# Conversions further behind their loads, and the first gated weights loaded in part, in a fused attention, expert and gated-MLP kernel

## The chip, the cores and the metric

The kernel runs on one core of a Trainium2 chip. The metric is the device time of one execution in microseconds, the median of several runs. Engines are named as in the profile: PE is TensorE (matmuls), PEld its weight loads, DVE VectorE, ACT ScalarE, POOL GpSimd (`G` in the code), SP SyncE, whose queue issues nearly all DMAs. Every engine works through its own queue in program order.

## What is computed

```python
state = f[:, :, t, :, None] * state + np.einsum('bhd,bhe->bhde', k[:, :, t], v[:, :, t])   # f = sigmoid(f_logit), 768 steps
y[:, :, t] = np.einsum('bhd,bhde->bhe', q[:, :, t], state)                                 # 4 batches, 8 heads of 48
...
x = attn_out.transpose(0, 2, 1, 3).reshape(B * S, H * D)            # 3072 tokens of 384
expert_idx = np.argmax(logits, axis=1)                              # 8 experts, cosine logits / tau
gate_w = probs[np.arange(N), expert_idx]
out[mask] = gate_w[mask, None] * (np.maximum(x[mask] @ w1[e], 0.0) @ w2[e])   # 384 -> 1024 -> 384
...
return ((x @ w_a) * (x @ w_b) @ w_out).astype(np.float32)           # 384 -> 1536 -> 384
```

All of it is in fp32. The inputs of the last step arrive as 64-bit floats.

## The kernel before

A product in fp32 is made of three matmuls: each operand is split into a high part (a rounded copy, on ACT) and a low part (the difference, on POOL or DVE), and the products high x high, low x high and high x low are added in PSUM. There are three stages. Attention and routing take the first 145 us or so; the tokens are scattered to slots in order of their expert.

**The expert loop** (L1367 on) runs `s` from 0 to 63: 8 experts of 8 steps (`FJ`). A step makes a block of hidden units (`h_part(s)`: 9 matmuls on lines 1212 to 1214, then `hh` on ACT and `hl` on DVE), adds the block of two steps before to the output (`y_part(s - 2)`: 9 matmuls, L1255) and, three times per expert, transposes tokens of the next one (`x_turn`, L1202; the two parts of `a` on ACT L1205 and DVE L1206). After an expert's last block its output is copied from PSUM to `yT` (DVE L1271, ACT L1273); the next expert's first output matmul into the same PSUM bank waits for that. `w_more(s)` loads the experts' weights into `raw` (L878) and splits them (L886 to L895).

Beside this, `prep_run(s)` (L1096) prepares the gated MLP's weights a little at a time: first what `defer` has put down for this step, then `loads()`, then the two streams `combines()` and `conv()`, as far as a budget of microseconds goes.
- `conv()` turns 18 pieces of 768 KB from 64 to 32 bits: three of `w_out`, six of `w_a`, six of `w_b`, three of `w_out`. A piece takes ACT L948 and DVE L950, L951 (into `ct`), L954 and a last operation (L957 or L987). `loads()` loads a piece into a free part of `big` and notes the step from which it may be converted. Converted `w_out` is split (ACT L963, POOL L964) and stored to `wost` (L969).
- `combine(0)` and `combine(1)` make 15 combined blocks each of `w_a` and `w_b` (sums on DVE L999; a scheme that needs 23 and not 27 block products), split them (ACT L1032, POOL L1035) and store them to `wst` in DRAM (L1055).

**The visits** (L1528 on): `P = at // 8` runs over the units of the gated MLP, 8 per tile of 512 tokens. A unit reads two chunks of `wst` (1024 and 896 KB, `w_chunk`, L1075), which go through a ring of three buffers `WR`; the ring lies in the two weight tiles of the last experts' ring that the last expert's pieces use first. A visit is 6 matmuls (L1456; `c2` has 3) and one or two additions of PSUM into `big` (DVE L1466, L1469, L1472, or ACT). Half of the visits of a unit fall into the next P (`late` in `SLOTS`), so P0 reads only nine of the fifteen rows: 0, 1 and 4 to 7 of chunk 0, and 2 to 4 of chunk 1. From P3 on the matmuls with `w_out` (L1485, L1487, L1489) run between the visits; their left operand is the product a * b (DVE L1433, split by ACT L1437 and POOL L1438). `x_prep` makes the 15 sums of x for a tile of tokens (L1347, split on L1355 and L1360): the first tile's within the last steps of the expert loop, on DVE, the others in the visits, on POOL. The gates (L1288 to L1311: a power on POOL, then short DVE operations) need the logits, which one DMA of 40-byte rows brings (L1542). The last two `y_part` run at visits 0 and 1. Every third visit calls `prep_run(64 + at // 3)`.

## Time and profile before

| what | value |
|---|---|
| median of 3 runs | 818.62 us (815.15 to 819.36) |
| the profiled execution | 818.64 us |
| its span, first to last instruction | 816.6 us |
| mean granted clock of TensorE | 0.984 of 2.4 GHz |
| busy: PE, PEld | 772.1 us (95%), 742.9 us |
| busy: DVE, ACT, POOL | 596.9 (73%), 420.5 (52%), 412.4 us (51%) |
| DMA | 226.8 MB, 278 GB/s over the span |

The span is one execution by the profiler; the time is that of the same execution and about 2 us longer. A timeline row gives the start, the length (of a group that runs together) and, in brackets, how long the engine was idle before it and what ended that. For SP the length of a group holds the waits between its issues. A stretch's `PEclk` is the mean granted clock: 1.00 is 2.4 GHz, 0.50 is 1.2 GHz.

### The profile page before, as it was taken

How to read it: one execution, taken by the hardware profiler on the slowest of the kernel's cores; microseconds unless marked ns; L12 is line 12 of the kernel's file. 1: busy time of each engine (PE TensorE's matmuls, PEld its weight loads, DVE VectorE, ACT ScalarE, POOL GpSimd, SP SyncE). 2: the span in 40 equal slices, each digit the busy share in tenths (PEclk: the TensorE clock that was granted, in tenths of full speed). 3: DMA queues.
4: the chain of work that ended last, by engine and by line, in shares of the span. 5: the costliest groups of instructions: out<-in, count | busy, mean ns of one | idle time of the engine just before them, and what ended most of it. 6: DMA issues, size and time to landing. Idle time of an engine off the chain costs nothing.

```text
span 816.6 us, 16783 instructions
## 1 busy us (share of the span) xinstructions
PE 772.1 (95%) x6354; PEld 742.9 (91%) x6354; DVE 596.9 (73%) x1007; ACT 420.5 (52%) x889; POOL 412.4 (51%) x392
## 2 busy tenths in 40 slices
PE   7899989789999999997899999999999999999995
PEld 5899988779989999996789999999999999999994
DVE  7999995689878957784798657866756765686552
ACT  5899973555657656643344344443434433444331
POOL 6667763353578746960455253436316535333313
PEclk9999999889999999998999999999999999999999
DMA  7989742988489987967998899789888888988982
GB/s 276 334 286 338 247 155 92 290 262 272 164 239 293 304 265 199 270 192 221 345 379 299 318 324 329 277 322 334 292 303 328 309 293 318 335 293 295 334 316 67
DMA packets 83087, 226.82 MB, mean 278 GB/s; under 512 B 10649, under 2 KB 42247, under 8 KB 76727
## 3 DMA queue, kind: packets, MB, share of 16 engines
q1 hardware_dynamic: 79639, 216.10, 78.3%
q0 software_dynamic: 3072, 9.56, 3.0%
q8 instruction: 52, 0.85, 0.4%
q14 instruction: 36, 0.29, 0.1%
q10 hardware_dynamic: 288, 0.02, 0.0%
HBM read 192.95 MB, written 32.70 MB: 276 GB/s over the span
## 4 chain that ended last, share of the span: by engine, by line
PE 61%; DVE 20%; DMA 9%; issue 5%; POOL 2%; ACT 2%; SPq 0%; DVEq 0%; POOLq 0%; ACTq 0%
PE pv L1456 20%; PE po L1255 8%; PE pw L1456 5%; PE pq L1489 5%; PE pq L1487 5%; PE pq L1485 5%; DMA raw<-moe_w 4%; DMA w<-wst 2%; PE ph L1212 2%; DVE Rt L241 2%; PE ph L1214 2%; PE ph L1213 2%; DVE big L1472 2%; DVE big L1433 2%; DVE a L1355 2%
## 5 line engine op out<-in xcount | busy, mean ns | idle before, releaser
L1438 POOL TENSOR_TENSOR w<-big,w 128x512 fp32r<-128x512 f32 x72 | 94.2, 1321 | 176.6 <-ACT w L1437 172.3
L1456 PE MATMUL pv<-w,w 128*128 128x256 f32 x912 | 136.6, 285 | 12.4 <-DMA w<-wst 6.9
L1472 DVE TENSOR_TENSOR big<-big,pv 128x512 f32<-128x512 f32 x144 | 98.3, 683 | 60.9 <-PE pv L1456 60.8
L1456 PEld LDWEIGHTS pv<-w,w 128*128 128x128 f32 x912 | 127.1, 190 | 17.0 <-DVE big L1466 5.2
L1456 PE MATMUL pv<-a,w 128*128 128x256 f32 x816 | 122.1, 283 | 0.2
L1456 PEld LDWEIGHTS pv<-a,w 128*128 128x128 f32 x816 | 115.0, 189 | 1.8 <-DVE big L1466 1.0
L895 POOL TENSOR_TENSOR w<-raw,w 128x512 fp32r<-128x512 f32 x48 | 78.4, 1654 | 42.2 <-ACT w L892 41.8
L1489 PE MATMUL pq<-raw,w 128*128 128x384 f32 x288 | 97.1, 337 | 1.6 <-POOL w L1438 1.6
L1485 PE MATMUL pq<-raw,w 128*128 128x384 f32 x288 | 97.2, 337 | 0.0
L1487 PE MATMUL pq<-raw,w 128*128 128x384 f32 x288 | 96.8, 336 | 0.0
L1255 PE MATMUL po<-hh,w 128*128 128x224 f32 (+7 forms) x384 | 84.7, 357 | 5.1 <-DVE yT L1271 4.2
L1466 DVE TENSOR_TENSOR big<-big,pv 128x256 f32<-128x256 f32 x96 | 40.3, 420 | 50.7 <-PE pv L1456 48.9
L1255 PEld LDWEIGHTS po<-hh,w 128*128 128x128 f32 x384 | 69.7, 199 | 7.7 <-DVE yT L1271 4.9
L1433 DVE TENSOR_TENSOR big<-big 128x512 f32<-128x512 f32 x72 | 65.3, 934 | 1.7
L1212 PE MATMUL ph<-a,w 128*128 128x224 f32 (+7 forms) x192 | 66.2, 345 | 0.0
L1214 PE MATMUL ph<-a,w 128*128 128x224 f32 (+7 forms) x192 | 65.9, 343 | 0.0
L1213 PE MATMUL ph<-a,w 128*128 128x224 f32 (+7 forms) x192 | 65.9, 343 | 0.0
L1437 ACT ACTIVATE w<-big 128x512 fp32r<-128x512 f32 x72 | 44.9, 633 | 38.7 <-DVE big L1433 38.7
L1463 ACT ACTIVATE big<-pw 128x256 f32<-128x256 f32 x48 | 18.4, 383 | 78.7 <-PE pw L1456 73.9
L1235 ACT ACTIVATE hh<-ph 128x224 fp32r<-128x224 f32 (+7 forms) x64 | 31.4, 491 | 49.7 <-PE ph L1214 49.4
L1489 PEld LDWEIGHTS pq<-raw,w 128*128 128x128 f32 x288 | 54.2, 188 | 2.2 <-POOL w L1438 2.2
L1485 PEld LDWEIGHTS pq<-raw,w 128*128 128x128 f32 x288 | 54.4, 189 | 0.6 <-ACT w L1437 0.6
(275 smaller groups left out, 1732.2 us busy)
## 6 DMA issues: line engine op xcount, KB each, us to landing
w<-wst SPq DMA_DIRECT2D x49, 1024.0 KB
w<-wst SPq DMA_DIRECT2D x49, 896.0 KB
raw<-wost SPq DMA_DIRECT2D x72, 384.0 KB
raw<-moe_w SPq DMA_DIRECT2D x32, 768.0 KB
qkf<-qkf SPq DMA_DIRECT2D x20, 768.0 KB
wst<-big SPq DMA_DIRECT2D x21, 512.0 KB
vx<-vx SPq DMA_DIRECT2D x24, 192.0 KB
big<-moe_w_out SPq DMA_DIRECT2D x6, 768.0 KB
```

The source lines that it names most:

```text
L895: (G if i < NPOOL else V).tensor_tensor(out=wt[:, 1, f], in0=raw[:, f], in1=wt[:, 0, f].bitcast(F32), op=ALU.subtract)
L1212: T.matmul(out=out, lhsT=wh, rhs=xh, start=first, stop=False)
L1213: T.matmul(out=out, lhsT=wl, rhs=xh, start=False, stop=False)
L1214: T.matmul(out=out, lhsT=wh, rhs=xl, start=False, stop=last)
L1255: T.matmul(out=OS[e][k], lhsT=w[:, j % 4, k * 128:(k + 1) * 128], rhs=x, start=(j == 0 and w is wh and x is hh), stop=(j == FJ - 1 and x i ...
L1433: V.tensor_tensor(out=a, in0=a, in1=b, op=ALU.mult)
L1438: G.tensor_tensor(out=g[:, 1], in0=a, in1=g[:, 0].bitcast(F32), op=ALU.subtract)
L1456: T.matmul(out=out, lhsT=wt, rhs=xt_, start=first and j == 0, stop=j == 2, skip_group_check=True)
L1472: V.tensor_tensor(out=o, in0=o, in1=bank, op=ALU.subtract)
L1485: T.matmul(out=q, lhsT=gh, rhs=wh, start=(f == 0), stop=False)
L1487: T.matmul(out=q, lhsT=gh, rhs=wl, start=False, stop=False)
L1489: T.matmul(out=q, lhsT=gl, rhs=wh, start=False, stop=(f == F2J - 1))
```

## The change

- `loads()`: a piece may be converted 5 steps after its load in the first expert, 3 in the others and 8 (of three visits each) in the visits, in place of 3 everywhere.
- Converted `w_out`: split and store one step later in the loop (2 and 3 steps behind). The last three pieces are split into tiles of the `a` ring that are free by then and not into a part of `big`, and the two pauses of 9 us of budget behind each are gone.
- The last three pieces of `w_out` may be loaded when `combine(1)` comes to its last block (phase 3.5), not when it has ended.
- `combine` ends two steps behind its last block and not three.
- `w_chunk(0)` loads six rows (768 KB, two DMAs) at s = 60, `w_chunk(1)` three rows (384 KB) at s = 62, each ahead of the step's `h_part`; chunk 2 is loaded whole after `combine(1)`, as before. Before, all three were loaded whole at that point.
- `x_prep` makes its sums two ahead of the split in place of one. The first tile's runs two per step from s = 57 and one in each visit, not three per step from s = 58.
- The gate logits are loaded at visit 9, not 2; the gates run on even visits 22 to 40, not 16 to 34.

```diff
-                if not at or (waiting[0] == (2, 1) and phase[0] < 4):
+                if not at or (waiting[0] == (2, 1) and phase[0] < 3.5):
...
-                ready.append((now[0] + 3, i) + waiting.pop(0))
+                ready.append((now[0] + (5 if now[0] < FJ else 3 if now[0] < NE * FJ else 8), i) + waiting.pop(0))
...
-                    to = part[n if n < 3 else 5].bitcast(F32R).rearrange("p (i j d) -> p i j d", i=2, j=2)
+                    to = (part[n].bitcast(F32R) if n < 3 else flat(X[NE - 1][n % 2])).rearrange("p (i j d) -> p i j d", i=2, j=2)
...
-                    defer(1, split)
-                    defer(2, store)
+                    lag = 2 if now[0] < NE * FJ else 1
+                    defer(lag, split)
+                    defer(lag + 1, store)
                     take(i, 2)
-                    if n >= 15:
-                        for _ in range(2):
-                            yield 9.0
...
             for i in range(NR):
+                if (w, i) == (1, NR - 1):
+                    free[5], phase[0] = now[0] + 1, 3.5
...
-            until = now[0] + 3
+            until = now[0] + 2
...
         def w_chunk(h):
-            if h < 2 * (NTT * NU + 1):
+            if h < 2:
+                for lo, hi in ((0, 2), (4, 8)) if h == 0 else ((2, 5),):
+                    SP.dma_start(out=WR[h][:, lo:hi].bitcast(F32), in_=wst[h, :, lo:hi])
+            elif h < 2 * (NTT * NU + 1):
...
-            for h in range(3):
-                w_chunk(h)
+            w_chunk(2)
...
             sums(0)
+            sums(1)
...
-                sums(o + 1)
+                sums(o + 2)
...
         for s in range(NE * FJ):
             e, j = divmod(s, FJ)
+            if s in (NE * FJ - 4, NE * FJ - 2):
+                w_chunk((s + 4 - NE * FJ) // 2)
...
-            if s == IDS + 1:
+            if s == IDS:
                 x_more()
-            if s > IDS:
-                for _ in range(3):
+            if s >= IDS:
+                for _ in range(2):
                     next(x_first, None)
...
+                next(x_first, None)
-            if at == 2:
+            if at == 9:
                 SP.dma_start(out=idf, in_=heads[0:NT].rearrange("(t p) w -> p t w", p=128))
-            if at == 16:
+            if at == 22:
...
-            if at >= 16 and at % 2 == 0 and at <= 34:
+            if at >= 22 and at % 2 == 0 and at <= 40:
```

How this moves instructions shows at three places. (Line numbers of the changed kernel are up to six higher; numbers behind names tell buffers apart.) The first is DVE's queue in the first expert, around the flag `flag_b`; `ct` and `big` are the two halves of a conversion, `a` the transposed tokens, `w` a weight split. Before:

```order
L1236 SCALAR_TENSOR_TENSOR hl<-ph,hh 128x224
L950 TENSOR_SCALAR ct<-ct 128x768
L951 TENSOR_SCALAR ct<-ct 128x768
L1162 TENSOR_REDUCE fl_94<-srt 1x1
L1163 TENSOR_SCALAR fl_94<-fl_94 1x1
L1164 TENSOR_SCALAR fl_94<-pcs 1x1
L1165 TENSOR_REDUCE flag_i<-fl_94 1x1
L1166 CAST flag_b<-flag_i 1x1
L1206 TENSOR_TENSOR a_2541<-pt,a_2540 128x448
L1236 SCALAR_TENSOR_TENSOR hl<-ph,hh 128x224
L954 SCALAR_TENSOR_TENSOR big<-big,ct 128x768
L957 SCALAR_TENSOR_TENSOR big<-big 128x768
```

and now, from `flag_b` on:

```order
L1169 CAST flag_b<-flag_i 1x1
L1209 TENSOR_TENSOR a_2541<-pt,a_2540 128x448
L1239 SCALAR_TENSOR_TENSOR hl<-ph,hh 128x224
L887 TENSOR_TENSOR w_2524<-raw,w_2524 128x512
L1209 TENSOR_TENSOR a_2541<-pt,a_2540 128x448
L1239 SCALAR_TENSOR_TENSOR hl<-ph,hh 128x224
L951 TENSOR_SCALAR ct<-ct 128x768
L952 TENSOR_SCALAR ct<-ct 128x768
L1209 TENSOR_TENSOR a_2541<-pt,a_2540 128x448
L1239 SCALAR_TENSOR_TENSOR hl<-ph,hh 128x224
L955 SCALAR_TENSOR_TENSOR big<-big,ct 128x768
L958 SCALAR_TENSOR_TENSOR big<-big 128x768
```

The first half of the first conversion, which stood ahead of the first `a`, stands behind the second, and its second half behind the third. From the first `a` to the copy of the first output `yT`, 18 rows further on, there are two whole conversions now and there were two and a half.

The second is DVE's queue ahead of the copy of expert 1's output (`yT`, 432 columns). Before, and then now:

```order
L1236 SCALAR_TENSOR_TENSOR hl<-ph,hh 128x416
L999 TENSOR_TENSOR yT_2534<-yT_2534,yT_2532 128x512
L999 TENSOR_TENSOR yT_2533<-yT_2532,yT_2534 128x512
L954 SCALAR_TENSOR_TENSOR big<-big,ct 128x768
L895 TENSOR_TENSOR w_66<-raw,w_66 128x512
L1236 SCALAR_TENSOR_TENSOR hl<-ph,hh 128x416
L1264 TENSOR_LOAD off_i
L1264 ISA x2
L1271 ISA
L1271 COPY yT_2533<-po 128x432
```

```order
L1034 TENSOR_TENSOR big<-yT_2533,big 128x4x128
L895 TENSOR_TENSOR w_66<-raw,w_66 128x512
L1239 SCALAR_TENSOR_TENSOR hl<-ph,hh 128x416
L1267 TENSOR_LOAD off_i
L1267 ISA x2
L1274 ISA
L1274 COPY yT_2533<-po 128x432
L998 TENSOR_TENSOR yT_2534<-yT_2534,yT_2532 128x512
L998 TENSOR_TENSOR yT_2533<-yT_2532,yT_2534 128x512
L955 SCALAR_TENSOR_TENSOR big<-big,ct 128x768
```

The two sums (L999, now L998) stood ahead of the copy and stand behind it.

The third is SP's queue at the end of the expert loop: stores of b's sums to `wst`, loads of chunks (`w_2524<-wst`, elements per partition), of 64-bit pieces (`moe_w_out`), of converted `w_out` (`raw<-wost`) and of the logits (`heads`). Before:

```order
L1055 DMA wst<-big 128x3x256
L1055 DMA wst<-big 128x256
L1055 DMA wst<-big 128x4x256
L1075 DMA w_2524<-wst 128x2048
L1075 DMA w_2524<-wst 128x1792
L1075 DMA w_2524<-wst 128x2048
L1428 DMA raw<-wost 128x768 x2
L1542 DMA yT_2534<-heads 128x24x10
L925 DMA big<-moe_w_out 128x2x768
L1075 DMA w_2524<-wst 128x1792
L1075 DMA w_2524<-wst 128x2048
L1075 DMA w_2524<-wst 128x1792
```

and now:

```order
L1076 DMA w_2524<-wst 128x512
L1076 DMA w_2524<-wst 128x1024
L1054 DMA wst<-big 128x3x256
L1054 DMA wst<-big 128x256
L926 DMA big<-moe_w_out 128x2x768
L1054 DMA wst<-big 128x4x256
L1076 DMA w_2524<-wst 128x768
L1079 DMA w_2524<-wst 128x2048
L926 DMA big<-moe_w_out 128x2x768
L1433 DMA raw<-wost 128x768 x2
L1079 DMA w_2524<-wst 128x1792
L1079 DMA w_2524<-wst 128x2048
```

Three loads in part (512 and 1024, then 768) stand among the stores, two conversion loads stand ahead of chunk 3 (1792), and the logits have gone behind chunk 4 (2048); behind that come two stores to `wost`, a third conversion load and the logits, and only then chunk 5.

## Rows read from the trace of the kernel before

**Rows 1.** The page, busy us, share of the span and instructions of TensorE.

```profile
PE 772.1 (95%) x6354; PEld 742.9 (91%) x6354; DVE 596.9 (73%) x1007; ACT 420.5 (52%) x889; POOL 412.4 (51%) x392
```

**Rows 2.** Busy us by stretch: PE, PEld, DVE, ACT, POOL, granted clock, DMA.

```profile
460.00:800.00 340.00, 339.66 (x2502) 337.03 (x2501) 223.46 (x368) 137.18 (x287) 139.46 (x128) 1.00 0.86 310
```

**Rows 3.** Waits of PE, whole run: us in total, times, longest.

```profile
PE pv L1456 <- DMA w<-wst: 6.9, 2, 4.7
PE pt L1202 <- DVE a L1206: 5.3, 3, 3.7
PE po L1255 <- DVE yT L1271: 4.2, 2, 3.1
```

**Rows 4.** PE's timeline: start, length, line, operation, [idle before <- releaser].

```profile
159.80 1.01 PE L1202 MATMUL pt<-ident,yT 112*128 112x112 f32 x4 [3.66 <-DVE a L1206]
178.89 2.23 PE L1255 MATMUL po<-hh,w 128*128 128x448 f32 x5 [3.14 <-DVE yT L1271]
...
241.59 1.22 PE L1255 MATMUL po<-hh,w 128*128 128x416 f32 x5 [1.06 <-DVE yT L1271]
```

**Rows 5.** DVE's timeline, 156 to 179 us.

```profile
156.31 0.56 DVE L950 TENSOR_SCALAR ct<-ct 128x768 f32<-128x768 f32 x1 [1.59 <-ACT ct L948]
156.91 1.65 DVE L951 TENSOR_SCALAR ct<-ct 128x768 int32<-128x768 int32 x1
...
159.14 0.60 DVE L1206 TENSOR_TENSOR a<-pt,a 128x448 fp32r<-128x448 f32 x1
...
159.97 0.94 DVE L954 SCALAR_TENSOR_TENSOR big<-big,ct 128x768 int32<-128x768 int32 x1
160.94 0.96 DVE L957 SCALAR_TENSOR_TENSOR big<-big 128x768 int32<-128x768 int32 x1
...
178.46 0.38 DVE L1271 COPY yT<-po 128x224 f32<-128x224 f32 x1
```

**Rows 6.** ACT's timeline, the split of the raw piece.

```profile
165.75 0.63 ACT L886 ACTIVATE w<-raw 128x512 fp32r<-128x512 f32 x1 [0.71 <-DMA raw<-moe_w]
```

**Rows 7.** Busy us by stretch, the three at low clock (columns as rows 2).

```profile
158.50:165.30 6.80, 5.50 (x27) 5.50 (x28) 6.24 (x15) 4.23 (x10) 1.86 (x1) 0.51 0.89 196
...
376.90:383.70 6.80, 6.16 (x21) 6.19 (x22) 0.00 (x0) 0.60 (x1) 0.00 (x0) 0.50 0.94 374
394.00:397.40 3.40, 3.40 (x19) 3.40 (x18) 1.41 (x3) 0.38 (x1) 0.00 (x0) 0.51 0.97 405
```

**Rows 8.** PE's timeline, end of the expert loop and first visits.

```profile
367.51 1.31 PE L1255 MATMUL po<-hh,w 128*128 128x384 f32 x6 [0.82 <-ACT hh L1235]
...
377.54 1.62 PE L1456 MATMUL pv<-w,w 128*128 128x256 f32 x6 [4.67 <-DMA w<-wst]
...
393.42 0.59 PE L1456 MATMUL pv<-w,w 128*128 128x256 f32 x3 [2.20 <-DMA w<-wst]
...
403.24 0.98 PE L1456 MATMUL pv<-w,w 128*128 128x256 f32 x6 [1.58 <-DVE big L1466]
...
404.77 0.88 PE L1456 MATMUL pv<-w,w 128*128 128x256 f32 x6
```

**Rows 9.** SP's timeline: issues, their length with the waits among them.

```profile
354.99 14.94 SPq L1055 DMA_DIRECT2D wst<-big  x6
370.02 6.08 SPq L1075 DMA_DIRECT2D w<-wst  x3
...
442.07 4.07 SPq L969 DMA_DIRECT2D wost<-big  x2
```

**Rows 10.** DMA packets, 376 to 382 us.

```profile
DMA packets 410, 2.40 MB, mean 400 GB/s; under 512 B 47, under 2 KB 47, under 8 KB 260
```

**Rows 11.** Busy us, first to sixth P with output matmuls (columns as rows 2).

```profile
404.77:452.57 47.80, 44.67 (x317) 41.95 (x316) 43.77 (x73) 23.08 (x50) 25.91 (x23) 1.00 0.92 340
```

**Rows 12.** DVE's and POOL's timelines, two operations of the gates.

```profile
400.57 1.83 DVE L1291 TENSOR_TENSOR yT<-yT,gm 128x192 f32<-128x192 f32 x1
...
388.75 4.56 POOL L1288 TENSOR_TENSOR gm<-yT,half 128x24 f32<-128x24 f32 x1 [19.22 <-DMA yT<-heads]
```

More of the change, by code (lines that the diff above doesn't have):

```diff
@@ L904, in build @@
         now = [0]
+        flat = lambda t: t.rearrange("p a b -> p (a b)")
         due, tail = [], []
@@ L1316, in build @@
         QS = {}
-        flat = lambda t: t.rearrange("p a b -> p (a b)")
         XS = [flat(wring[2 + i // 6])[:, (i % 6) * 512:(i % 6 + 1) * 512] for i in range(12)]
```

## The prediction

> **What bounds the kernel now.** I read the page first: TensorE is busy 772.1 of 816.6 us [rows 1], so nearly all a change can win lies in the 44 us in which it isn't, and in the stretches where it runs at half clock. The table by stretches shows where that isn't: from 460 us on TensorE is busy 339.66 of 340 us at full clock [rows 2]. Whatever the change does to the work there is worth nothing unless it makes another engine the bound. So I looked at the waits of TensorE over the whole run [rows 3]: the longest single ones are for a chunk of gated weights (4.7), for the transposed tokens `a` (3.7) and for the output copy `yT` (3.1). The timelines put each in its place [rows 4, 8]. Last, the granted clock around them: after the stalls at 156 and 373 us TensorE ran at 1.2 GHz for 6.8 us each, and again for 3.4 us at 394 [rows 7]. A stretch at half clock loses half its length: 3.4, 3.4 and 1.7 us. The profiled execution took 818.64 us, its span 816.6; the median of the three runs is 818.62, so sums against the profiled one need no correction. Anything under 0.5% (4.1 us) can't be told from no change here.
>
> **First conversion two steps later (157 to 179 us).** DVE's in-order queue holds the first conversion's two `ct` operations (0.56 and 1.65 us) ahead of the first `a` copy, and they could only start at 156.31 because their piece had just landed [rows 5]. TensorE waits 3.66 us for that copy [rows 4]. In the new order both stand behind two `a` copies, so this stall goes, and with it the half-clock stretch (3.4). That is 7.1 us at 165 us, but not at the end: the next hard point is the first matmuls of expert 1's output, which wait for the copy of expert 0's `yT` at 178.46 [rows 4, 5]. Between `a` and that copy DVE still does two whole conversions in place of two and a half (0.94 and 0.96 us go, and some waiting on ACT), and one weight split that needs a raw piece which lands at 165.75 [rows 6] whatever DVE does, since its load was issued long before. From 159.14 to 178.84 are 19.7 us; from an `a` copy at about 156.0 (when its transposes are done; ACT's half of the copy stands behind the same conversion now) I take off the 1.9 us and some 1.1 of the waits, but keep 0.5 for the landing: 156.0 + 17.2 + 0.5 = 173.7, TensorE restarts at 174.3 instead of 178.89. TensorE will have come there early and still stalls, for about as long as now, so I count no gain of clock there. **Term: -4.5** (-3 if the split waits longer on the raw piece, -6 if the copy comes as soon as DVE's work allows).
>
> **Expert 1's copy ahead of two sums (241 us).** TensorE's 1.06 us wait for `yT` [rows 4] ends behind two sums of the combination that now stand behind the copy. **Term: -1.1** (0 to -1.1: the same time may come back as a wait for weights).
>
> **End of the expert loop (367 to 405 us).** Now: TensorE finishes its outputs at 372.87 and waits 4.67 us for chunk 0 [rows 8], which SP issued only at 370.02, after the last store of b's sums [rows 9]. From 372.87 to the first visit with output matmuls at 404.77 are 31.9 us. Of these 4.67, 2.20 and 1.58 are the stalls [rows 8], 5.1 half of 6.8 and 3.4 at half clock [rows 7]: 18.35 us are left, the work at full clock. After: chunk 0's six rows go at the sixtieth step of the loop, when SP has the last but one group of b stores out, and chunk 1's three at the sixty-second; 768 KB at the 400 GB/s of [rows 10] is 2 us, so both are there when TensorE comes. That is at 372.05, since the 0.82 us wait at 367.51 [rows 8] (ACT's copy behind x preparation) goes with x prepared two steps instead of three per turn. What is late next is chunk 3. Chunk 2 still has to wait for the last store of b: its issue ended at 369.93, and SP stood with the three chunk loads until 376.10 [rows 9], so about 5.9 us to land. Behind chunk 2 in SP's new order come a 768 KB conversion load, two of 384 KB and chunk 3 with 896 KB: 3.54 MB at 400 GB/s from 375.8 is 384.6. TensorE wants it after its two outputs, P0 and half of P1, about 10 of the 18.35 us: 382. So 2.6 us of wait, and I add 1.4 for chunk 5, which now stands behind a pair of stores, the third conversion load and the gate logits: 372.05 + 18.35 + 4.0 = 394.4 for what is now at 404.77. **Term: -10.4.** Bounds: -14.4 with no new wait, -7 if the waits are twice mine less some overlap, or another half-clock stretch follows.
>
> What a store costs before its bytes can be read has a rival price. The Trainium skill, "DMA: Bandwidth & Descriptors", section on the anatomy of one DMA, fits a DMA (on GpSimd's path) as 2.0 us plus the bytes at 436 GB/s; for the last 512 KB store that estimate is 3.2 us where this trace shows 5.9. By the page chunk 2 would go 2.7 us sooner, chunk 3 would not be late, and the sum would be that of rival 2 below.
>
> **Visits with output matmuls, until DVE is rid of conversions (405 to 453 us).** DVE is busy 43.77 of 47.80 us there, TensorE 44.67 [rows 11]: DVE sets the pace. Two conversions lie in it now, one of them after the change (the second is done ahead): 0.56 twice, 0.94 and 0.96 [rows 5], 3.0 us less (with both `ct` operations at the cheap price; 1.65 is the dear one). Against it the gates, six visits later, bring their dear product of 1.83 us [rows 12] into it, with its short neighbours some 2.2 more. **Term: -0.9** (+3 if the pile of gates and third conversion holds one more visit, -3 if the gates find room).
>
> Moved at no cost: GpSimd's power for the gates (4.56 us, [rows 12]), six or seven visits later, with nobody waiting for it in that stretch; split copies of converted w_out into spare `a` tiles; x sums two ahead. Were their cover gone, that is GpSimd held by the power, they cost up to 4.6 us of late `w` splits, which is in the +3 end above and the slower rival.
>
> **Sum:** 4.5 + 1.1 + 10.4 + 0.9 = 16.9; 818.64 - 16.9 = **801.7**. Its own range, with the ends above partly cancelling, is 797 to 807.
>
> **Rivals.** (1) *DMA takes half of the late gain.* Chunks 3 and 5 come 5.2 us (half of 10.4) later than I said, and expert 1's output restarts at 176.8 and not 174.3, 2.5 more. For it: in 376 to 382 us the DMA engines already move 400 GB/s with no rest [rows 10]. Against it: 0.8 MB of chunks 0 and 1 is no longer loaded at all, and the other 1.1 MB goes two to four steps earlier. 801.7 + 7.7 = 809.4. (2) *Stores land sooner* now that no chunk load shares the queue with the last of them: chunk 3 comes in time and its 2.6 us go, 799.1. For it: what landed in 5.9 us had 1.9 MB of chunk loads on its heels, and now has 0.4. Against it: most of those loads can only have moved once the store was through. (3) *It does not do what it says*: chunk 0's part stands on SP until all stores of b have landed, as it does now, so the 10.4 goes; and expert 1's output waits for the raw piece until 178.9, so the 4.5 goes: 816.6. Against it: the rows it reads were stored by earlier steps. (4) *Slower: SP is held by the stores of converted w_out.* SP issues in order; such a pair held it 4.07 us at 442.07 [rows 9], when GpSimd was late with the split. In the new order pairs stand ahead of chunk 5, chunk 7 and a later one, with GpSimd's 4.56 us power in between. A chunk that is issued 4.07 late needs 2.3 us to load (896 KB at 400 GB/s) with TensorE waiting, and 1.7 of half clock after it: 8.1 us each, 24.2 for three, 825.9. It decides from 7.0 us each on (21 us, up to 822.7). Against it: in the new order the first two splits on GpSimd come right after the last split of the sums, ahead of the power, so only the third can be late.
>
> **How the numbers follow.** Forecast 0.54 (801.7); (1) 0.20 (809.4); (2) 0.10 (799.1); (3) 0.10 (816.6); (4) 0.06 (825.9). Faster by over 0.5% (under 814.5) is the first three: 0.84; the same 0.10; slower 0.06. The range reaches from 796 to 814: it takes in the forecast's own range, (1) and (2) but for their tails, and leaves out (3) and (4) and about 0.04 below.
>
> **What would show it.** Right: the wait of TensorE for `a` at 156 us is under 0.5 us, the one for `yT` stays between 3 and 4.5 us and ends at 173 to 176; the 241 us wait is gone; chunk 0 has landed before TensorE ends the outputs; the first output matmul of the visits starts 15 to 20 us earlier than now in the trace (10.4 + 5.6); waits for `w<-wst` are left, on chunks 3 and 5, 2 to 5 us in all; the distance from 404.77 to 452.57 is 47 us, and from there to the end unchanged. Wrong: the chunk waits add up to over 8 us, or DVE's stretch grows by over 4, or half clock turns up in a new place.

## The result: 0.65% slower

| | before | after |
|---|---|---|
| median of 20 runs each | 818.22 us (814.67 to 819.58) | 823.62 us (817.22 to 827.04) |
| ratio of the runs | | 1.0065, 95% interval 1.0046 to 1.0084 |
| the profiled execution, its span | 818.64, 816.6 us | 824.94, 822.9 us |

The forecast was 801.7 us, the range 796 to 814. The page of the changed kernel, TensorE's busy time and its clock in 40 slices:

```profile
PE 774.3 (94%) x6354; PEld 744.5 (90%) x6354; DVE 602.5 (73%) x1007; ACT 419.9 (51%) x889; POOL 406.5 (49%) x392
...
PEclk9999999989999999999898999999999999999999
```

TensorE's waits over the whole run (us in all, times, longest):

```profile
PE pv L1461 <- DMA w<-wst: 6.1, 1, 6.1
PE pv L1461 <- DVE big L1477: 5.6, 4, 3.3
PE po L1258 <- ACT yT L1276: 5.1, 2, 4.9
PE pv L1461 <- DVE big L1471: 4.7, 4, 2.9
...
PE pt L1205 <- DVE a L1209: 2.1, 1, 2.1
```

Against [rows 3] the waits for `a` have gone from 5.3 to 2.1 us, and two kinds stand at the top that were small: TensorE waits for DVE's additions (L1471, L1477), that is for a free bank. The timeline of TensorE has them, with the wait in brackets:

```profile
174.69 1.82 PE L1258 MATMUL po<-hh,w 128*128 128x448 f32 x3 [4.93 <-ACT yT L1276]
...
281.44 0.56 PE L1205 MATMUL pt<-ident,rows 100*128 100x100 f32 x4 [2.08 <-DVE a L1209]
...
373.93 0.98 PE L1461 MATMUL pv<-w,w 128*128 128x256 f32 x6 [0.82 <-DVE hl L1239]
...
398.69 0.98 PE L1461 MATMUL pv<-w,w 128*128 128x256 f32 x3 [6.10 <-DMA w<-wst]
...
412.14 1.32 PE L1461 MATMUL pv<-w,w 128*128 128x256 f32 x6 [2.91 <-DVE big L1471]
...
434.37 1.01 PE L1461 MATMUL pv<-w,w 128*128 128x256 f32 x3 [3.35 <-DVE big L1477]
```

[Rows 4] answer to the first, [rows 8] to the third and fourth. Behind each of these waits but that of 0.82 at 373.93 the clock falls (busy us by stretch, columns as in rows 2; the granted clock is the third number from the end):

```profile
174.69:181.00 6.31, 6.31 (x17) 5.28 (x18) 6.21 (x7) 2.46 (x5) 4.25 (x3) 0.54 1.02 304
283.00:288.00 5.00, 5.00 (x20) 4.91 (x20) 4.45 (x7) 1.70 (x5) 0.99 (x1) 0.67 0.90 184
398.60:402.10 3.50, 3.42 (x16) 3.45 (x17) 1.72 (x3) 0.63 (x2) 0.00 (x0) 0.50 0.95 299
412.00:416.00 4.00, 3.86 (x17) 3.86 (x18) 2.40 (x6) 1.02 (x3) 2.57 (x4) 0.57 0.08 32
434.00:438.00 4.00, 3.63 (x15) 3.63 (x16) 2.09 (x5) 0.66 (x2) 1.09 (x2) 0.50 0.78 288
```

For the places I take the starts of TensorE's matmuls on both timelines: first of a step of the expert loop, first of a P.

| us | before | after | forecast for the change |
|---|---|---|---|
| attention, up to step 0 | 145.2 | 144.4 | 0 |
| step 0 to step 33 | 119.6 | 117.7 | |
| step 33 to step 63 | 104.3 | 107.7 | (both rows) -5.6 |
| step 63 to P0 | 8.4 | 4.2 | |
| P0 to P3 | 27.2 | 28.9 | (both rows) -10.4 |
| P3 to P8 | 47.8 | 55.7 | -0.9 |
| P8 to the last matmul | 356.6 | 356.8 | 0 |

In the 17 profiles of this document step 0 starts at 143.3 to 146.9 us, though no edit aims at attention, so later places are best compared from step 0 on.

Of the 16.9 us forecast, 2.5 came at the end of the loop and 1.9 in its first half; the second half gave back 3.4, and P3 to P8, where I had put a fraction of a microsecond, took 8.

### The profile page after: what moved, and what is told of

Its sections match the earlier page's. It is cut to its first block, busy times and chain, and to the rows that moved or that the text cites. A ratio compares the mean times of both kernels' runs of the same rounds, so it can differ in the third digit from the quotient of the medians.

```text
span 822.9 us, 16788 instructions
## 1 busy us (share of the span) xinstructions
PE 774.3 (94%) x6354; PEld 744.5 (90%) x6354; DVE 602.5 (73%) x1007; ACT 419.9 (51%) x889; POOL 406.5 (49%) x392
## 3 DMA queue, kind: packets, MB, share of 16 engines
q0 software_dynamic: 3072, 9.56, 3.0%
## 4 chain that ended last, share of the span: by engine, by line
PE 55%; DVE 28%; DMA 6%; issue 5%; ACT 4%; POOL 2%; SPq 0%; DVEq 0%; ACTq 0%; POOLq 0%
PE pv L1461 20%; PE po L1258 6%; PE pw L1461 5%; PE pq L1494 5%; PE pq L1492 5%; PE pq L1490 5%; DMA raw<-moe_w 3%; DVE Rt L241 3%; DVE Bt L230 3%; DVE big L1438 2%; PE ph L1215 2%; PE ph L1216 2%; PE ph L1217 2%; DVE qc L249 2%; DVE a L1357 2%
## 5 line engine op out<-in xcount | busy, mean ns | idle before, releaser
L1477 DVE TENSOR_TENSOR big<-big,pv 128x512 f32<-128x512 f32 x144 | 98.2, 683 | 68.9 <-PE pv L1461 68.2
L1258 PE MATMUL po<-hh,w 128*128 128x224 f32 (+7 forms) x384 | 82.6, 349 | 7.4 <-ACT yT L1276 5.1
L1471 DVE TENSOR_TENSOR big<-big,pv 128x256 f32<-128x256 f32 x96 | 40.2, 419 | 51.0 <-PE pv L1461 47.7
L1258 PEld LDWEIGHTS po<-hh,w 128*128 128x128 f32 x384 | 67.0, 191 | 10.7 <-ACT yT L1276 5.8
L1438 DVE TENSOR_TENSOR big<-big 128x512 f32<-128x512 f32 x72 | 67.3, 962 | 1.7
```

Source lines behind the costliest of these rows:

```text
L1258: T.matmul(out=OS[e][k], lhsT=w[:, j % 4, k * 128:(k + 1) * 128], rhs=x, start=(j == 0 and w is wh and x is hh), stop=(j == FJ - 1 and x i ...
L1438: V.tensor_tensor(out=a, in0=a, in1=b, op=ALU.mult)
L1477: V.tensor_tensor(out=o, in0=o, in1=bank, op=ALU.subtract)
```

## The experiments

Theory Q, the first: the logits' 3072 small packets, queued behind 3 MB, hold SP, chunk 5 comes late, and TensorE loses the wait and a stretch at half clock behind it. Its rivals: B, the bytes ahead of chunk 5; G, the gates' place itself. All ratios are to runs of the kernel before on the same chip; "stage" times are starts as in the table above, from one profile each.

**Logits through GpSimd's queue.**

```diff
-                SP.dma_start(out=idf, in_=heads[0:NT]...
+                G.dma_start(out=idf, in_=heads[0:NT]...
```

> The changed kernel with one DMA moved from SP's queue to GpSimd's: the load of the gate logits (3072 rows of 40 bytes) at visit 9. In the changed kernel SP stood 9.44 us on chunk 5, the next DMA behind it, and TensorE waited 6.10 us for that chunk. Theory Q (the many small packets, behind some 3 MB that are still queued, keep SP from handing over anything more): SP's issue of chunk 5 takes under 1.5 us, TensorE's wait for it falls below 1.5 us, the first visit of P3 starts at 394 to 397 instead of 402.87, and the time is 812 to 818. Rival B (chunk 5 is late because of the bytes ahead of it, whoever issues the logits): the wait stays above 4 us and the time at 821 to 826.

Measured: 822.65 us, ratio 1.0047 (1.0016 to 1.0077). SP's timeline in the changed kernel, its issue of chunk 5 (start, length):

```profile
384.78 9.44 SPq L1079 DMA_DIRECT2D w<-wst  x1
```

The same row of this run:

```profile
388.30 0.33 SPq L1079 DMA_DIRECT2D w<-wst  x1
```

TensorE's wait for that chunk in this run:

```profile
401.49 0.76 PE L1461 MATMUL pv<-w,w 128*128 128x256 f32 x2 [4.21 <-DMA w<-wst]
```

So the hold is real (9.44 us against 0.33), and it is a small part of the cost: from the start of P1 (381.34 and 385.19) TensorE has its chunk after 16.30 us where it was 17.35. The bytes ahead are the same, and the chunk waits for them either in the queue or in front of it. What the hold adds shows in the rate of the DMA engines of the changed kernel from 380 to 400 us (GB/s, 40 slices of half a us):

```profile
GB/s 412 406 406 430 430 500 387 416 401 420 328 295 262 229 328 426 263 406 399 411 406 415 396 394 182 110 105 27 6 119 72 272 387 416 401 369 328 279 279 262
```

They run dry from 392 on, and fill again after the issue ends at 394.22. Q falls as the main cause, B fits.

**Gates and logits back in their place.**

```diff
-            if at == 9:
+            if at == 2:
-            if at == 22:
+            if at == 16:
-            if at >= 22 and at % 2 == 0 and at <= 40:
+            if at >= 16 and at % 2 == 0 and at <= 34:
```

> The changed kernel with the gates where they were: logits loaded at visit 2, gates on even visits 16 to 34. Theory Q: the logits now stand ahead of chunk 3 with less queued before them; SP is held there for 2 to 5 us, TensorE waits 1 to 4 us for chunk 3 and not for chunk 5, and DVE's 2.86 us wait for GpSimd's power at 410 is gone, since the power runs while GpSimd has nothing else: P8 starts 6 to 11 us earlier than 458.61, time 812 to 818. Rival B: only DVE's wait goes, P8 2 to 4 us earlier, 819 to 822.

Measured: 818.22 us, ratio 0.9987 (0.9971 to 1.0004). This one edit undone takes back the whole loss, and what is left of the change is worth nothing measurable. P3 to P8 is 46.3 us (55.7 with the late gates). TensorE's timeline has chunk 3 and chunk 5 late, by more than I had:

```profile
388.24 0.74 PE L1461 MATMUL pv<-w,w 128*128 128x256 f32 x3 [3.26 <-DMA w<-wst]
...
399.17 0.98 PE L1461 MATMUL pv<-w,w 128*128 128x256 f32 x3 [3.81 <-DMA w<-wst]
```

**The gates' late place alone, on the kernel before** (the same edit, forwards).

> The kernel before with the sixth part of the change alone: logits loaded at visit 9, gates on even visits 22 to 40. Theory Q: the small packets come behind queued chunk and conversion loads, the next chunk load on SP is held for 4 us or more, TensorE waits for it and half clock follows; and GpSimd's power (4.6 us) falls among the splits of P3: 4 to 10 us slower than before, 822 to 829. Rival (the gates' place costs nothing without the loads in part ahead of it): 816 to 820.

Measured: 821.12 us, ratio 1.0027 (1.0002 to 1.0053), between the two. P3 to P4 takes 14.1 us there and took 8.9, but P0 to P3 is 3.9 shorter: the logits, before, stood ahead of chunk 3. P4 to P6 does not suffer (18.3 us, 19.0 before), so the loss there in the changed kernel needs more than the gates' place.

**Logits loaded at visit 2, gates still late** (the first line of that edit alone).

> The changed kernel with the logits loaded at visit 2 again, but the gates still on visits 22 to 40. It parts the two halves of that edit. Theory G (most of the loss comes from the gates' place: DVE waits for GpSimd's 4.6 us power among the splits of P3, and the gates' short operations meet the third conversion in P4 to P6): the wait of TensorE for a chunk in P2 is 3 to 4.5 us, the waits for DVE in P3 to P6 stay at 6 us or more, time 820 to 823. Rival L (it comes from the load at visit 9): time 817 to 819.

Measured: 823.64 us, ratio 1.0051 (1.0030 to 1.0073). Theory G: the load's place is worth nothing that can be told from these runs (1.0051 and 1.0065), the gates' place is what costs. TensorE's timeline has the two waits of the changed kernel:

```profile
410.51 1.27 PE L1461 MATMUL pv<-w,w 128*128 128x256 f32 x6 [2.90 <-DVE big L1471]
...
432.73 1.01 PE L1461 MATMUL pv<-w,w 128*128 128x256 f32 x3 [3.34 <-DVE big L1477]
```

POOL's timeline in the changed kernel shows the first of them being made:

```profile
402.56 2.54 POOL L1443 TENSOR_TENSOR w<-big,w 128x512 fp32r<-128x512 f32 x2 [11.53 <-ACT w L1442]
405.06 4.67 POOL L1291 TENSOR_TENSOR gm<-yT,half 128x24 f32<-128x24 f32 x1
409.72 1.25 POOL L1443 TENSOR_TENSOR w<-big,w 128x512 fp32r<-128x512 f32 x1
```

and DVE's:

```profile
409.77 1.24 DVE L1296 TENSOR_SCALAR gm<-gm 128x24 f32<-128x24 f32 x1 [2.86 <-POOL gm L1291]
...
411.27 0.82 DVE L1471 TENSOR_TENSOR big<-big,pv 128x256 f32<-128x256 f32 x2
```

The power (L1291) takes 4.67 us on GpSimd. DVE's next gate operation (L1296, 24 columns) needs its result and waits 2.86 us at the head of DVE's queue; behind it stand the additions of L1471, and TensorE needs the bank that they free. The power starts at 405.06 now, and L1296 could have run at 406.9, where DVE's wait begins. Before, the power started at 388.75 and took 4.56 us [rows 12]: it was done at 393.31. Its reader is this row of DVE's timeline of the kernel before, 11.7 us later, so there was room for it:

```profile
405.03 0.17 DVE L1293 TENSOR_SCALAR gm<-gm 128x24 f32<-128x24 f32 x1
```

The operation of 1.83 us at 400.57 in [rows 12] is the subtraction ahead of that reader; it does not use the power.

**The power alone at visit 12**, the logits loaded at visit 2, and the other gate operations from visit 24.

```diff
-            if at >= 22 and at % 2 == 0 and at <= 40:
+            if at == 12 or at >= 24 and at % 2 == 0 and at <= 40:
```

> As the run with the logits loaded back at visit 2 (823.64 us), and of the gates' operations the first alone, GpSimd's power of 4.6 us, at visit 12 instead of 22; DVE's gate operations stay on visits 24 to 40. Theory G1 (the gates' late place costs through the power: it stands between GpSimd's splits of the first product in P3, and DVE's next gate operation waits for it in front of the additions that free TensorE's banks): TensorE's 2.9 us wait in P3 and the half clock behind it go, P3 to P4 falls from 13.2 to 8.5 to 9.5 us, time 818 to 820.5. The second loss, 3.3 us in P5, stays. Rival G2 (DVE's own gate operations are what is too much in P3 to P6): P3 to P4 stays over 11 us, time 822.5 to 824.5.

Measured: 821.40 us where the kernel before had 820.39, ratio 1.0002 (0.9985 to 1.0019), against 1.0051: 4.0 us. P3 to P4 is 9.0 us. So the first wait is the power's, and the second stays (TensorE's timeline):

```profile
431.60 0.63 PE L1461 MATMUL pv<-w,w 128*128 128x256 f32 x3 [3.34 <-DVE big L1477]
```

**The third conversion behind the gates as well**, on top of that: the third piece is loaded at turn 75 and converted three turns behind its load, and its split goes to another free part.

```diff
-                if not at or (waiting[0] == (2, 1) and phase[0] < 3.5):
+                if not at or (waiting[0] == (2, 1) and phase[0] < 3.5) or (waiting[0] == (2, 3) and now[0] < NE * FJ + 11):
-                ready.append((now[0] + (5 if now[0] < FJ else 3 if now[0] < NE * FJ else 8), i) + waiting.pop(0))
+                ready.append((now[0] + (5 if now[0] < FJ else 3), i) + waiting.pop(0))
```

> As the run with GpSimd's power at visit 12 (ratio 1.0002, P4 to P6 24.0 us of which 3.3 a wait for DVE and half clock behind it), with the third piece of w_out loaded at turn 75 and converted three turns later, behind the last gate operation and not among them; its split goes to the free part of big. Nothing is left out. Theory D (what is left of the loss in P4 to P6 is DVE's in-order queue: the third conversion's 3 us and the gates' short operations fall into the same two P, while GpSimd's splits make DVE's operations longer): the 3.3 us wait before P6 goes, P4 to P6 falls to 19 to 21 us, P6 to P8 grows by 1 to 2.5 us, time 816.5 to 819. Rival (the products of those P alone are too much for DVE): the wait stays above 2 us, 820 to 822.

Measured: 813.51 us against 820.61, ratio 0.9914 (0.9884 to 0.9945). P4 to P6 is 17.1 us (24.0 without, 19.0 before the change), P6 to P8 18.8 (17.6). The wait in P5 goes with the third conversion and its split; the last section shows which part of it made the wait. More was won than I expected: P4 to P6 falls by 6.9 us where I had 3 to 5, and P2 to P3 falls from 9.9 to 7.5 us, where the piece's 768 KB are no longer loaded in P1.

**Bytes of w_out out of P1 and P2** (gates in their old place).

```diff
-                if not at or (waiting[0] == (2, 1) and phase[0] < 3.5):
+                if not at or (waiting[0] == (2, 1) and phase[0] < 3.5) or (waiting[0] == (2, 3) and now[0] < NE * FJ + 8):
-                ready.append((now[0] + (5 if now[0] < FJ else 3 if now[0] < NE * FJ else 8), i) + waiting.pop(0))
+                ready.append((now[0] + (5 if now[0] < FJ else 3), i) + waiting.pop(0))
-                    defer(lag + 1, store)
+                    defer(lag + (5 if n in (15, 16) else 1), store)
```

> The changed kernel with the gates back, and with the bytes of the last w_out pieces taken out of P1 and P2: the two pairs of stores of converted w_out four turns (twelve visits) later, the third piece loaded at turn 72 instead of 65, converted 3 turns behind its load. Nothing is left out. Theory S (chunk loads of P1 to P3 wait for the bytes queued ahead of them: 0.8 MB of stores, 0.8 MB of conversion load): TensorE's waits for w<-wst, 7.1 us in the run with the gates back, fall to 2 to 4 us; P3 starts 3 to 6 us earlier relative to P0; time 812 to 816. Rival (DVE bounds P0 to P8 whatever the DMA does): chunk waits fall, but P8 is as far from P0 as before (75 us), time 817 to 820.

Measured: 812.50 us, ratio 0.9921 (0.9892 to 0.9950), where the same without this edit had 0.9987. P0 to P3 goes from 29.0 to 24.1 us. The needless bytes are the cause: the changed kernel loads the third piece at 383.75, eight turns before it is converted, and stores 0.8 MB right ahead of chunk 5. The third conversion runs later in this run too, but that wins nothing where it runs: P3 to P8 takes 47.3 us and took 46.3. TensorE's waits for chunks are 4.9 us (7.1 without the edit), more than the 2 to 4 that I expected.

**The same, with the logits through GpSimd's queue at visit 2.**

> As the run with late w_out bytes, and the logits are loaded through GpSimd's queue at visit 2 (as 48 larger packets in the earlier run, not 3072 of 40 bytes). Theory S: the 2 us of small packets ahead of chunk 3 go too; waits for w<-wst fall below 2 us in all, P3 1 to 3 us earlier than without it, time 810 to 814. Rival (DVE bounds): 816 to 819.

Measured: 811.30 us, ratio 0.9910 (0.9878 to 0.9942), 0.1% from the run before and inside its interval. The chunk waits are 4.5 us and not under 2; the longest, 3.09, is for chunk 3.

**Late gates on top of the late bytes.**

> The run with late w_out bytes (812.5 us, ratio 0.9921) with the gates late again (visits 22 to 40; logits still loaded by SP at visit 2). Theory G: the price of the gates' late place is in the order on GpSimd and DVE, not in the DMA queue, so it is to be paid here too: P3 to P4 12 us or more (8.9 without), P0 to P8 8 to 11 us longer than 71.3, ratio 0.998 to 1.004. Rival (it only shows behind late chunks): P0 to P8 under 4 us longer, ratio 0.992 to 0.996.

Measured: 817.77 against 820.61 us, ratio 0.9962 (0.9940 to 0.9985), between the two. P0 to P8 is 6.5 us longer than without; the waits of 3.15 and 3.31 us for DVE in P3 and P5 are there as ever. The price of the gates' place does not hang on late chunks, though 0.4% is less than the 0.8% it costs in the changed kernel.

**Loads in part undone**, in the run with the gates back, and in the one with the late bytes:

```diff
-            if h < 2:
-                for lo, hi in ((0, 2), (4, 8)) if h == 0 else ((2, 5),):
-                    SP.dma_start(out=WR[h][:, lo:hi].bitcast(F32), in_=wst[h, :, lo:hi])
-            elif h < 2 * (NTT * NU + 1):
+            if h < 2 * (NTT * NU + 1):
...
-            w_chunk(2)
+            for h in range(3):
+                w_chunk(h)
...
-            if s in (NE * FJ - 4, NE * FJ - 2):
-                w_chunk((s + 4 - NE * FJ) // 2)
```

> The changed kernel with two parts undone: the gates' place (logits at visit 2, gates from visit 16), and the loads in part (chunks 0 to 2 whole, behind the last store of b). Against the run with only the gates back (818.22 us) this is what the loads in part are worth. In that run P0 came 4 us earlier than before, measured from step 63, but P8 was no earlier. Theory S (P1 to P3 are bound by bytes on the DMA queue, so what is won at P0 is given back by P3): P0 3.5 to 4.5 us later, P8 less than 1.5 us later, time 817 to 820. Rival (the 4 us at P0 are real and reach the end): 821.5 to 824.

> The run with late w_out bytes and the logits through GpSimd's queue (811.3 us), with the loads in part undone: chunks 0 to 2 whole, behind the last store of b. Theory S (the loads in part win 4 us at P0; with the full queue behind P0 they were given back, with the bytes out of the way they reach the end): P0 starts 4 to 5 us later after step 63, P8 3 to 5 us later, time 814.5 to 816.5. Rival (worth nothing either way): 810.5 to 812.5.

Measured: 819.38 us, ratio 1.0006 (0.9985 to 1.0027), against 0.9987; and 817.25 against 820.39 us, ratio 0.9967 (0.9948 to 0.9987), against 0.9910. With the queue full behind P0 the loads in part are worth 0.2%, less than the two intervals; with the bytes out of the way 0.6%, 4.7 us. The step from 63 to P0 is 4.4 to 4.5 us longer in both. The first run's profile does not show the giving back (its P8 is 5.1 us later after step 63), so that half rests on medians and is not shown by a trace.

**First expert's conversions 3 steps behind their loads again**, in the changed kernel, and with the late bytes:

> The changed kernel with a piece converted 3 steps after its load in the first expert too (was 5): the expert loop's conversions and sums stand two steps earlier again. Theory M (the two steps of delay win 2.7 us by expert 1's output but push sums and stores into the stretch 260 to 290 us, where 4.5 us are lost): the 3.66 and 3.14 us waits at 156 and 176 us come back, the loss at 260 to 290 goes, step 63 starts 1 to 3 us earlier than 369.79, and the time is 820 to 823. Rival: the loss at 260 to 290 comes from something else (the later split and store of converted w_out, the shorter end of combine): step 63 starts 2 to 3 us later, 825 to 828.

> The run with late w_out bytes and the logits through GpSimd's queue (811.3 us), with the first expert's conversions 3 steps behind their loads again and not 5. Theory M (what the two steps win in the first expert, 2.7 us, is gone by step 48, since DMA is busy all the time from 240 to 300 us and paces the weights there): step 12 starts 2 to 3 us later measured from step 0, step 48 less than 0.7 us later, time 810 to 813. Rival (the 2.7 us are kept): 813.5 to 815.

Measured: 820.65 us, ratio 1.0022 (1.0005 to 1.0038), against 1.0065; and 814.51 against 820.39 us, ratio 0.9932 (0.9913 to 0.9952), against 0.9910. In the four profiles with three steps (these two, before, and the late gates on before) steps 0 to 33 take 119.4 us on average and steps 33 to 48 54.4; in the 13 with five steps 117.6 and 57.1. So the two steps win 1.8 us by step 33 and lose 2.7 by step 48: what the first expert wins is given back inside the loop. That is not the end of it. From step 48 to step 63 these two runs take 54.4 and 54.3 us and the other 15 take 50.4 to 50.8; a wait for `hl` of 3.40 and 3.18 us stands at the end of the loop there. Counted from step 0, step 63 comes 1.8 us later in the first and 3.2 later in the second than with five steps and all else the same. The 0.4% that the first of the two wins all the same is won behind the loop: its P3 to P8 takes 48.3 us and not 55.7, with a wait before P6 of 0.84 us and not 3.35. Beside the late bytes nothing can be told at the end. What exactly is late between 260 and 290 us, and what makes `hl` late, no run here shows.

**Later still.** The second conversion load at turn 67 and the first two rows of w_out at visit 14:

> The run with late w_out bytes and the logits through GpSimd's queue (811.3 us), with two more things taken from ahead of chunk 3: the second conversion load at turn 67 (visit 9 and on) instead of 64, and the first two rows of converted w_out (384 KB each, needed in P3) loaded at visit 14 instead of 0. Nothing is left out. Theory S: the last chunk wait of 3.1 us, in P1, goes, with the half clock behind it if there is any: P1 to P2 falls from 10.6 to about 7 us, time 806.5 to 809.5. Rival (the same bytes come later and make chunk 5 or 7 late instead): waits for w<-wst stay at 3 us or more, 810 to 813.

Measured: 817.89 against 820.39 us, ratio 0.9970 (0.9950 to 0.9990). One part is not computed as in the others: the last pieces' splits fall so late that they overwrite part of the sums of x for the second tile; the operations and their order are all there. P1 to P2 is 7.0 us as expected, P2 to P4 24.5 and not 14.5. The chunk waits are 3.6 us, as the rival had it, but the time is 5 us over the rival's too: waits for DVE's additions of 1.86, 2.15 and 2.44 us have come in P3 and P5.

**The two rows alone later**, on the run with the late bytes and the logits through GpSimd's queue.

```diff
-        for n in range(2):
-            wo_load(n)
...
+            if at == 14:
+                for n in range(2):
+                    wo_load(n)
```

> The run with late w_out bytes and the logits through GpSimd's queue (811.3 us, ratio 0.991), with the first two rows of converted w_out loaded at visit 14 and not at 0; the conversions stay. Theory S: 0.8 MB less ahead of chunk 3, so its 3.1 us wait falls to 1 to 1.5 us, P1 to P2 from 10.6 to 7.5 to 9 us, ratio 0.988 to 0.990 (about 809.5). Rival: chunk 5 gets the wait instead, ratio 0.990 to 0.993.

Measured: 811.25 against 820.61 us, ratio 0.9892 (0.9860 to 0.9923). P1 to P2 is 8.5 us, the chunk waits 2.1 us in two. Its page:

```profile
PE 767.2 (95%) x6354; PEld 737.0 (91%) x6354; DVE 598.2 (74%) x1007; ACT 419.7 (52%) x889; POOL 408.6 (51%) x393
```

The span is 807.1 us: TensorE is busy 4.9 us less than before the change [rows 1], since less of its work runs at half clock (mean granted clock 0.990 where it was 0.984), and idle 39.9 us where it was 44.5. This is the lowest ratio of all runs, though its interval overlaps those of the two runs with the late bytes, and it is faster than both kernels: the change without the gates' new place, with the logits through GpSimd's queue and the bytes of w_out where nothing waits behind them. From step 63 to P8 it takes 74.0 us where the kernel before took 83.4: 9.4 of the 11.3 us forecast for the end of the loop and the visits. Most of what is missing of the 16.9 is the 5.6 of the loop.

## Why the prediction was wrong

Three terms miss by about as much each: P3 to P8 (-0.9 forecast, +7.9 measured), the end of the loop (-10.4 and -2.5) and the loop before it (-5.6 and +1.4). The first turns a gain into a loss; with the gates alone put back the ratio is 0.9987, no loss and no gain. The other two are why no gain is left.

**The step that failed** is "Moved at no cost: GpSimd's power for the gates (4.56 us, [rows 12]), six or seven visits later, with nobody waiting for it in that stretch". Somebody waits for it everywhere: its reader is DVE's next gate operation, and what counts is the distance to that, not the engine's leisure. I had counted the gates' operations as 2.2 us of DVE's work. P3 to P8 takes 8 us more: 4.3 at P3 to P4 (a wait of 2.91 and half clock behind it) and 5.9 at P4 to P6 (3.35 and half clock), less 2.3 won at P6 to P8, where a conversion has gone. With the gates back it takes 46.3 us, so their place costs 9.4 there; of the 3.0 put down for the conversion that has gone, 1.5 is won (46.3 against 47.8). With the power early the first wait is gone, with the conversion moved too the second. The end "+3" of that term was the bound of one event, and two came, each with a stretch at half clock that the term did not have.

**End of the loop: -10.4 forecast, -2.5 measured.** The first half was right: chunk 0's part is there, P0 starts 4.2 us earlier after step 63 (4.67 and 0.82 foreseen; a wait of 0.82 for `hl` stays). What is late next I named, chunk 3 and chunk 5, with 4.0 us in all. P0 to P3 takes 28.9 us, and it adds up: the 18.35 of work, 6.10 of wait for chunk 5 (chunk 3 is in time here), 1.75 for 3.5 us at half clock behind it, and 2.4 of waits for DVE's additions (0.47, 1.02, 0.93), which I had taken out with the 1.58 of [rows 8]; together 28.6. The mis-sized term is chunk 5: "I add 1.4 for chunk 5", where 0.8 MB of stores and 0.8 MB of a conversion that nobody needed yet stand ahead of it, 3.9 us at 400 GB/s, and the hold behind the small packets, about 1 more. That sum was there to be made. With the logits back ahead of chunk 3 the same bytes make two waits, 3.26 and 3.81, and 29.0 us. Rival 1 had the mechanism with 5.2 us.

**First conversion: -4.5 forecast.** The 3.66 us wait is gone, and the place of the next was right: expert 1's output restarts at 174.69 (174.3 forecast; 0.8 of the 4.2 us won there is attention, which ends earlier in this profile). The reason was right in part. ACT does wait for the raw piece, until 164.94, but the copy that ends TensorE's wait is ACT's own and no longer DVE's: it stands behind a conversion of ACT that waits 3.12 us for DVE. ACT's timeline of the changed kernel:

```profile
164.94 0.63 ACT L886 ACTIVATE w<-raw 128x512 fp32r<-128x512 f32 x1 [6.35 <-DMA raw<-moe_w]
...
171.98 0.96 ACT L949 ACTIVATE ct<-big 128x768 f32<-128x768 f32 x1 [3.12 <-DVE big L955]
...
174.25 0.63 ACT L1276 ACTIVATE yT<-po 128x224 f32<-128x224 f32 x2
```

DVE's copy, the last before the change [rows 5], runs when TensorE has restarted:

```profile
174.97 0.38 DVE L1274 COPY yT<-po 128x224 f32<-128x224 f32 x1
```

That 174.3 came so close is in part luck. The sum counts the 0.5 for the landing twice (19.7 less 1.9 and 1.1 is 16.7, not 17.2) and has TensorE restart 0.6 after the copy's end, where the rows of before have 0.05; without the two it is near 173.3.

That it stalls "for about as long as now, so I count no gain of clock there" was too kind: TensorE comes earlier, waits 4.93 us and not 3.14, and is at a mean clock of 0.54 for 6.3 us after it, where it was slow for 3.5. Counted from step 0, there are 1.9 us left by step 12 of the 6.2 at step 9. **Expert 1's copy: -1.1** (of 432 columns: by the count of the term before it is expert 2's) was right at its place: the 1.06 us wait at 241 is gone, with a like one of 1.04 at 209 in its stead. Neither reaches P0; the stretch around 281 us, with a wait of 2.08 and a mean clock of 0.67 for 5 us in this profile, takes both back. The prediction has no term for that stretch.

**Rival 4** had the right sign and the wrong mechanism. SP was indeed held, by the logits and not by stores, and that cost about 1 us.

## What to carry to other kernels

Before an operation is moved on a slow engine, find its reader and what stands behind the reader in that engine's queue: an in-order queue hands a wait of one small operation to everything behind it. When a start is brought forward, add up the bytes queued ahead of each later transfer up to the point where the queue runs empty, and move those that nobody needs yet. Each wait of 2.1 to 6.1 us in the changed kernel's trace above had a stretch at lower clock behind it that cost 1.7 to 2.9 us more; a forecast has to price the two together.

## What the runs showed of the hardware

A DMA issue is not always short. SP's issue of chunk 5 took 9.44 us behind 3072 queued rows of 40 bytes and 0.33 us without them; through GpSimd's queue the same rows took 1.52 us of GpSimd's time to issue. The DMA engines had run dry when it ended. No run here says why it was held.

A DVE operation beside one of GpSimd took twice as long here, and more. POOL's timeline in the changed kernel:

```profile
429.19 1.87 POOL L965 TENSOR_TENSOR a<-big,a 128x768 fp32r<-128x768 f32 x1
```

and DVE's around it:

```profile
425.06 1.29 DVE L1438 TENSOR_TENSOR big<-big 128x512 f32<-128x512 f32 x2
...
427.14 0.94 DVE L1357 TENSOR_TENSOR a<-rows,a 128x256 fp32r<-128x256 f32 x1
...
429.62 1.99 DVE L1438 TENSOR_TENSOR big<-big 128x512 f32<-128x512 f32 x1
431.54 0.94 DVE L1357 TENSOR_TENSOR a<-yT,a 128x256 fp32r<-128x256 f32 x1
...
432.73 0.99 DVE L1314 TENSOR_TENSOR g<-g 128x24 f32<-128x24 f32 x1
...
435.02 0.42 DVE L1357 TENSOR_TENSOR a<-rows,a 128x256 fp32r<-128x256 f32 x1
```

The product of L1438 (0.65 us each where two stand in a group of 1.29) starts at 429.62 within POOL's 1.87 us split and ends at 431.61, 0.55 after the split's end at 431.06; the split of L1357 takes 0.94 beside POOL and 0.42 without. The Trainium skill, "SBUF — State Buffer", section "Who interferes with whom", says that a VectorE instruction with two SBUF inputs contends with a GpSimd instruction that reads SBUF, and that this contention for the shared ports is an exclusive lock. These rows agree.

How much of the wait before P6 this makes can be read from the run with the first expert's conversions three steps behind. It has the same late gates and the third conversion in P4 too, but GpSimd's split of the converted piece runs in P4 (P5 starts at 429.9 there, at 426.4 in the changed kernel) and not beside these operations. POOL's timeline of that run, then DVE's:

```profile
425.69 1.87 POOL L965 TENSOR_TENSOR a<-big,a 128x768 fp32r<-128x768 f32 x1 [6.24 <-ACT a L964]
```

```profile
433.05 0.85 DVE L1438 TENSOR_TENSOR big<-big 128x512 f32<-128x512 f32 x1
433.82 0.41 DVE L1357 TENSOR_TENSOR a<-yT,a 128x256 fp32r<-128x256 f32 x1
...
434.48 0.18 DVE L1314 TENSOR_TENSOR g<-g 128x24 f32<-128x24 f32 x1
```

In the changed kernel the same three operations take 1.99, 0.94 and 0.99 us, 2.5 more in all, and TensorE's wait is 3.35 us and not 0.84, 2.5 more. By this comparison most of that wait is GpSimd's work falling beside DVE's, and not the amount of DVE's own. No run moves the split alone.
